# Token lists of the expert slots: scatter and gather through a DRAM table, against indicator matrices summed on TensorE

## The chip, the cores and the metric

The kernel is one program on one core of a Trainium2 chip. The metric is the device time of one execution in microseconds (us). Three executions of the kernel before took 1595.52, 1600.85 and 1601.16 us; their median, 1600.85 us, is the time before.

## The reference

Three layers run one after the other on 8 x 576 = 4608 tokens. Only the third, a routed mixture of eight experts, bears on the change.

```python
def _moe2_ref(x, w_gate, w1, w2):            # x: 4608 x 512, 8 experts, F = 1024
    logits = x @ w_gate
    expert_idx = np.argmax(logits, axis=1)
    ...
    gate_w = probs[np.arange(N), expert_idx]
    for e in range(E):
        mask = expert_idx == e
        xe = x[mask]
        h = np.maximum(xe @ w1[e], 0.0)
        out[mask] = gate_w[mask, None] * (h @ w2[e])
...
x = _attn_ref(q, k, v)                       # block-causal attention, 8 heads
x = _moe_ref(x, w1, w2, w3, w_out)           # ((x @ w1) * (x @ w2)) @ w3 @ w_out
return _moe2_ref(x, moe2_w_gate, moe2_w1, moe2_w2)
```

## The kernel before

The program has three stages: attention with the first half of the dense layer; the rest of the dense layer with the routing (from about 884 to 1090 us of the trace); and the experts (to the end). The order of the instructions is the order in which the Python code issues them; each engine runs its own list in that order and waits on semaphores. DMAs are issued by SP (SyncE, `nc.sync`) and by POOL (GpSimd, `indirect_dma_start`), each a list in program order too.

**Routing stage.** The tokens are taken in nine groups of four tiles of 128. `x2_bank` computes half a tile of the layer's output (24 float32 matmuls into one PSUM bank); ACT copies it to `row`, and `store_x2` writes finished rows to `x2d` in DRAM. `route` finds each token's expert (`oh`, a one-hot), its rank within the expert (two bf16 matmuls with `tri`, into `r`), and from both a position, expert times region plus rank (`posi`). Then it scatters the token numbers `tid` to these positions in four DRAM tables `tab`, one POOL DMA per tile, 36 in all, 4 bytes per token. The tables have been zeroed at the start of the program (`tab<-ti`).

**The held banks.** Eight banks of the last two groups (the `held` list) are kept back, so that TensorE has work while VectorE (DVE) does the last routing. They are called bank 0 to bank 7 here; each is followed by a 256 KB store to `x2d`. `slot_table` runs between them. It counts the tokens of each expert (`cnt`, one matmul), lays the experts out over 25 slots (18 of them pairs, with 256 tokens; 43 units of 128 in all), and makes `widx`, the index for the weights of each slot, and `ui`, the index of each unit's row in the tables. Then it gathers those rows back (`idr<-tab`, four POOL DMAs), transposes and sums them on TensorE (`p`), and writes the token numbers to `ids`.

**Experts.** For each slot, `wload` fetches 2 MB of weights by an indirect DMA with `widx` (`wr`), twice: number 2s for the first layer of slot s, 2s+1 for the second. `rload` gathers the slot's tokens from `x2d` by `ids` (tile `x`). `wsplit` splits the weights into a high part on ACT (`wh`) and a low part on DVE or POOL (`wl`). `xprep` transposes the tokens on TensorE (`t`) and splits them on ACT and DVE (`xhl`). Then TensorE multiplies (`hps`, `yps`), and the result is scattered to the output. The first slot is started in `run`, ahead of the loop.

Of the kernel before, what the change touches and what calls it, by code (L numbers as in the profile page):

```python
# [8 lines left out]
F32 = mybir.dt.float32  # L9
F32R = mybir.dt.float32r  # L10
BF16 = mybir.dt.bfloat16
# [35 lines left out]
def tile_moe_stack(ctx: ExitStack, tc: tile.TileContext, qd, kd, vd, w1, w2, w3t, wo, wg,  # L47
                   e1, e2, c_id, c_msk, c_tri, c_tid, c_row, c_cst, out):
# [11 lines left out]
    NUE = -(-NT // 256) * 2  # L60
    REG = NUE * 128
# [4 lines left out]
    tab = [dram.tile([9 * REG, 1], F32, name=f"tab{j}") for j in range(4)]  # L66
# [5 lines left out]
    one = const.tile([128, 128], F32, name="one")  # L72
    cst = const.tile([128, 16], F32, name="cst")
    crow = const.tile([128, c_row.shape[1]], F32, name="crow")
    tid = const.tile([128, NTILE], F32, name="tid")
# [78 lines left out]
    def attention(sa):  # L154
# [235 lines left out]
        for dst_, src in ((t2, c_tri), (tid, c_tid), (crow, c_row), (cst, c_cst)):  # L390
            nc.sync.dma_start(out=dst_, in_=src)
        NZ = 9 * REG // 128
        ti = ld.tile([128, max(NZ, RW)], F32, name="ti")
# [171 lines left out]
    def route(g, row, lg):  # L565
# [14 lines left out]
        oh = ws.tile([128, 4, 8], BF16, tag="oh", name="oh")[:, :nt]  # L580
# [3 lines left out]
        for j in range(nt):  # L584
# [14 lines left out]
        nc.vector.tensor_tensor(out=rk, in0=ps[:, :8 * nt].rearrange("p (a b) -> p a b", b=8),  # L599
                                in1=cst[:, 8:16].unsqueeze(1).to_broadcast([128, nt, 8]), op=ALU.add)  # L600
        nc.vector.tensor_tensor(out=rk, in0=rk, in1=oh, op=ALU.mult)
# [3 lines left out]
        nc.vector.tensor_copy(out=posi[:, :nt], in_=pos)  # L605
# [12 lines left out]
    def slot_table():  # L618
# [4 lines left out]
        t = ws.tile([U, 8 * NUE], F32, tag="t8", name="t8", bufs=1)  # L623
        v = ws.tile([U, 96], F32, tag="tv", name="tv", bufs=1)
        c8, u8, p8 = v[:, 0:8], v[:, 8:16], v[:, 16:24]
        nc.vector.tensor_copy(out=c8, in_=cnt[0:U, :8])
        t3 = t.rearrange("p (e s) -> p e s", s=NUE)
        nc.vector.tensor_tensor(out=t3, in0=c8.unsqueeze(2).to_broadcast([U, 8, NUE]),
                                in1=crow[0:U, 0:NUE].unsqueeze(1).to_broadcast([U, 8, NUE]), op=ALU.is_gt)
        nc.vector.tensor_reduce(out=u8, in_=t3, axis=AX.X, op=ALU.add)  # L630
        h = NUE // 2
        t4 = t[:, 0:8 * h].rearrange("p (e s) -> p e s", s=h)
        nc.vector.tensor_tensor(out=t4, in0=u8.unsqueeze(2).to_broadcast([U, 8, h]),
                                in1=crow[0:U, NUE:NUE + h].unsqueeze(1).to_broadcast([U, 8, h]), op=ALU.is_ge)
        nc.vector.tensor_reduce(out=p8, in_=t4, axis=AX.X, op=ALU.add)
        sc = ws.tile([U, 2, 24], F32, tag="sc", name="sc", bufs=1)
        nc.vector.memset(sc, 0.0)
        A = sc[:, :, 8:24]
        nc.vector.tensor_scalar(out=A[:, 0, 0:8], in0=p8, scalar1=2.0, scalar2=None, op0=ALU.mult)
        nc.vector.tensor_tensor(out=A[:, 0, 8:16], in0=u8, in1=A[:, 0, 0:8], op=ALU.subtract)  # L640
# [3 lines left out]
        ends = sc[:, 0, 8:24]  # L644
        starts = sc[:, 0, 7:23]
        bs = v[:, 24:40]
        co = crow[0:U, NUE + h:]
        nc.vector.tensor_copy(out=bs[:, 0:8], in_=co[:, 8:16])
        nc.vector.scalar_tensor_tensor(out=bs[:, 8:16], in0=p8, scalar=2.0, in1=co[:, 8:16], op0=ALU.mult, op1=ALU.add)
        nc.vector.tensor_tensor(out=bs, in0=bs, in1=starts, op=ALU.subtract)  # L650
        P2 = sc[:, 0, 15:16]
        tt = v[:, 40:48]
        nc.vector.scalar_tensor_tensor(out=tt[:, 0:1], in0=P2, scalar=0.5, in1=co[:, 17:18], op0=ALU.mult, op1=ALU.min)
        nc.vector.scalar_tensor_tensor(out=tt[:, 1:2], in0=P2, scalar=0.5, in1=co[:, 18:19], op0=ALU.mult,
                                       op1=ALU.is_le)
        nc.vector.tensor_tensor(out=tt[:, 0:1], in0=tt[:, 0:1], in1=co[:, 16:17], op=ALU.add)
        nc.vector.scalar_tensor_tensor(out=tt[:, 0:1], in0=tt[:, 1:2], scalar=1000.0, in1=tt[:, 0:1],
                                       op0=ALU.mult, op1=ALU.add)
        g0, g1 = v[:, 48:64], v[:, 64:80]
        tb = tt[:, 0:1].to_broadcast([U, 16])  # L660
        nc.vector.tensor_tensor(out=g0, in0=starts, in1=tb, op=ALU.is_le)
        nc.vector.tensor_tensor(out=g1, in0=ends, in1=tb, op=ALU.is_le)
        nc.vector.tensor_tensor(out=g0, in0=g0, in1=g1, op=ALU.subtract)
        nc.vector.tensor_tensor(out=bs, in0=bs, in1=tb, op=ALU.add)
        nc.vector.tensor_tensor(out=bs, in0=bs, in1=g0, op=ALU.mult)
        nc.vector.tensor_reduce(out=tt[:, 2:3], in_=bs, axis=AX.X, op=ALU.add)
        nc.vector.scalar_tensor_tensor(out=tt[:, 2:3], in0=g1[:, 15:16], scalar=float(8 * REG // 128),
                                       in1=tt[:, 2:3], op0=ALU.mult, op1=ALU.add)
        ui = ws.tile([U, 1], I32, tag="ui", name="ui", bufs=1)
        nc.vector.tensor_copy(out=ui, in_=tt[:, 2:3])  # L670
        g8 = v[:, 80:96]
        nc.vector.tensor_tensor(out=g8, in0=g0, in1=co[:, 19:35], op=ALU.mult)
        nc.vector.tensor_reduce(out=tt[:, 3:4], in_=g8, axis=AX.X, op=ALU.add)
        nc.vector.scalar_tensor_tensor(out=tt[:, 3:4], in0=g1[:, 15:16], scalar=7.0, in1=tt[:, 3:4],
                                       op0=ALU.mult, op1=ALU.add)
        dg = ws.tile([U, U], F32, tag="dg", name="dg", bufs=1)
        nc.vector.tensor_scalar(out=dg, in0=ident[0:U, 0:U], scalar1=tt[:, 3:4], scalar2=None, op0=ALU.mult)
        used = tt[:, 4:5]
        nc.vector.tensor_scalar(out=used, in0=P2, scalar1=0.5, scalar2=float(NPR), op0=ALU.mult, op1=ALU.min)
        nc.vector.tensor_tensor(out=used, in0=ends[:, 15:16], in1=used, op=ALU.subtract)  # L680
        nc.vector.tensor_copy(out=nuse, in_=used[0:1])
        ir = ws.tile([U, 4, 128], F32, tag="idr", name="idr", bufs=1)
        for j in range(4):
# [200 lines left out]
    with tc.manual_schedule():  # L884
# [140 lines left out]
        for i, h_ in enumerate(held):  # L1025
            x2_bank(*h_)
            store_x2(h_[0], h_[4], h_[1])
            if i == 0:
# [3 lines left out]
                for _ in rt:  # L1032
                    pass
# [85 lines left out]
```

## Time and profile before

| | us |
|---|---|
| median of three executions | 1600.85 |
| the profiled execution | 1599.49 |
| its span, from the first to the last instruction | 1597.7 |
| around the span | 1.8 |
| busy time of PE (TensorE) in the span | 1522.2 |
| busy time of DVE (VectorE) | 972.6 |
| busy time of ACT (ScalarE) | 885.2 |
| busy time of POOL (GpSimd) | 784.8 |

The busy times are sums over stages with different limits. Which engine sets the time of a stage is read from that stage: from its stretch of the windows and from the timelines of the engines there. The granted clock of TensorE has two levels, 2.4 GHz (1.00 in the profile) and 1.2 GHz (0.50).

### The profile page before, as it was taken

Reading aid. Unit: us, or ns where it says so; the run is one execution under the profiler, and the core shown is the slowest. Engines: PE = TensorE matmul, PEld = TensorE weight load, DVE = VectorE, ACT = ScalarE, POOL = GpSimd, SP = SyncE. Lnnn points to the kernel's source line nnn. Section 1 sums busy time; section 2 is a strip of 40 time slices with the busy share of each in tenths; the row PEclk is TensorE's granted clock in tenths of the full one; section 3 lists DMA queues with packets and bytes.
Section 4 is the critical chain, followed back from the end, with each engine's and each line's share of the span. In section 5 each row is a group of like instructions: output and inputs, shape, how many; then the busy total and the mean of one; then the engine's idle time right before and its main releaser. Section 6 shows DMA issues by size and latency. Waiting matters only on the chain. (4 is left out here: it accounts for less than half of the span.)

```text
span 1597.7 us, 28972 instructions
## 1 busy us (share of the span) xinstructions
PE 1522.2 (95%) x10689; PEld 1425.6 (89%) x10689; DVE 972.6 (61%) x2508; ACT 885.2 (55%) x1961; POOL 784.8 (49%) x768
## 2 busy tenths in 40 slices
PE   6888999999999999999999999994999999999996
PEld 3568999999999999999999999994998898898896
DVE  7777666666666666666569243351755766565761
ACT  5586766766676667666435233321644555555551
POOL 4577566566656565564224033233436454645441
PEclk9589999999999999999999999997999999999999
DMA  6523332333232323230464467739166425465240
GB/s 197 145 80 105 86 103 90 98 97 100 86 102 87 103 92 103 88 93 24 154 182 162 85 140 139 146 64 172 48 230 232 175 71 220 162 226 209 105 146 21
DMA packets 59059, 198.31 MB, mean 124 GB/s; under 512 B 10568, under 2 KB 11340, under 8 KB 55330
## 3 DMA queue, kind: packets, MB, share of 16 engines
q1 hardware_dynamic: 45026, 117.87, 27.7%
q0 software_dynamic: 13888, 78.54, 13.8%
q8 instruction: 87, 1.43, 0.4%
q14 instruction: 58, 0.48, 0.1%
HBM read 187.27 MB, written 39.24 MB: 142 GB/s over the span
## 5 line engine op out<-in xcount | busy, mean ns | idle before, releaser
L309 POOL TENSOR_SCALAR P<-P,m 128x512 f32<-128x512 f32 (+4 forms) x288 | 161.9, 563 | 223.0 <-DVE m L308 159.8
L79 DVE TENSOR_TENSOR wl<-wr,wh 128x1024 fp32r<-128x1024 f32 x128 | 219.5, 1741 | 63.3 <-ACT wh L78 44.3
L775 PE MATMUL hps<-xhl,wh 128*128 128x256 f32 x1152 | 207.9, 282 | 3.5 <-ACT xhl L756 2.1
L818 PE MATMUL yps<-wh,hhw 128*128 128x512 f32 x624 | 201.4, 398 | 3.4 <-DVE hhw L780 2.7
L294 DVE CUSTOM_DVE_ANT_0 P<-s,msk 128x512 f32<-128x512 f32 (+2 forms) x320 | 152.0, 482 | 86.4 <-PE t L326 52.6
L78 ACT ACTIVATE wh<-wr 128x1024 fp32r<-128x1024 f32 x168 | 169.8, 1061 | 50.9 <-DMA wr<-e,widx 50.9
L775 PEld LDWEIGHTS hps<-xhl,wh 128*128 128x128 f32 x1152 | 179.8, 190 | 5.7 <-ACT xhl L756 2.5
L302 ACT ACTIVATE P<-P,m 128x512 f32<-128x512 f32 (+4 forms) x288 | 166.8, 579 | 10.2 <-DVE m L294 8.2
L313 DVE TENSOR_TENSOR ptl<-t,pth 128x512 fp32r<-128x512 f32 (+3 forms) x288 | 146.2, 508 | 38.5 <-ACT pth L312 33.2
L775 PE MATMUL hps<-xhl,wl 128*128 128x256 f32 x576 | 163.2, 283 | 2.4 <-POOL wl L79 2.4
L556 PE MATMUL x<-wfh,abh 128*128 128x264 f32 (+1 forms) x576 | 163.4, 284 | 0.0
L556 PE MATMUL x<-wfl,abh 128*128 128x264 f32 (+1 forms) x576 | 162.8, 283 | 0.0
L556 PE MATMUL x<-wfh,abl 128*128 128x264 f32 (+1 forms) x576 | 162.3, 282 | 0.0
L464 ACT ACTIVATE ab<-mm 128x288 f32<-128x288 f32 x128 | 52.7, 411 | 184.9 <-PE mm L458 183.7
L326 PE MATMUL t<-ident,P 128*128 128x128 f32 x768 | 137.6, 283 | 12.9 <-DVE m L307 12.9
L818 PEld LDWEIGHTS yps<-wh,hhw 128*128 128x128 f32 x624 | 116.6, 188 | 32.5 <-DVE hhw L780 5.4
L356 PE MATMUL av<-ptl,VV 128*128 128x256 f32 (+1 forms) x448 | 127.6, 307 | 5.8 <-DVE m L307 5.0
L312 ACT ACTIVATE pth<-t 128x512 fp32r<-128x512 f32 (+3 forms) x288 | 129.4, 449 | 5.0 <-PE t L326 1.8
L356 PE MATMUL av<-pth,VV 128*128 128x256 f32 (+1 forms) x448 | 128.7, 305 | 0.7 <-ACT pth L312 0.7
L326 PEld LDWEIGHTS t<-ident,P 128*128 128x128 f32 x768 | 97.5, 145 | 28.3 <-issue 17.2
L818 PE MATMUL yps<-wl,hhw 128*128 128x512 f32 x312 | 122.7, 393 | 0.0
L780 DVE SCALAR_TENSOR_TENSOR hhw<-hps,hhw 128x512 fp32r<-128x512 f32 x72 | 49.6, 690 | 112.4 <-ACT hhw L779 107.7
(224 smaller groups left out, 4478.0 us busy)
## 6 DMA issues: line engine op xcount, KB each, us to landing
qr<-qd SPq DMA_DIRECT2D x29, 640.0 KB
abT<-ab SPq DMA_DIRECT2D x64, 288.0 KB
abr<-abT SPq DMA_DIRECT2D x36, 512.0 KB
kr<-kd SPq DMA_DIRECT2D x29, 576.0 KB
vr<-vd SPq DMA_DIRECT2D x32, 320.0 KB
str<-w SPq DMA_DIRECT2D x16, 512.0 KB
str<-w3t SPq DMA_DIRECT2D x16, 512.0 KB
x2d<-row SPq DMA_DIRECT2D x7, 1026.0 KB
```

What stands on the lines that cost most here:

```text
L78: nc.scalar.activation(out=hi, in_=src, func=AF.Copy)
L79: (eng or nc.vector).tensor_tensor(out=lo, in0=src, in1=hi.bitcast(F32), op=ALU.subtract)
L294: nc.vector.tensor_tensor_reduce(out=pr[:, o_:o_ + w_], in0=s_, in1=msk[:, c_:c_ + w_], scale=-0.125, scalar=BIG, op0=ALU.add, op1=ALU.min ...
L302: nc.scalar.activation(out=pr, in_=pr, func=AF.Exp, bias=m[:, 0:1], scale=-1.0, accum_out=m[:, 3:4])
L309: nc.gpsimd.tensor_scalar(out=pr, in0=pr, scalar1=m[:, 6:7], scalar2=1.0, op0=ALU.mult, op1=ALU.mult)
L312: nc.scalar.activation(out=dst_h, in_=src, func=AF.Copy)
L313: nc.vector.tensor_tensor(out=dst_l, in0=src, in1=dst_h.bitcast(F32), op=ALU.subtract)
L326: nc.tensor.transpose(t_[:, 128 * c:128 * c + 128], pr[:, 128 * c:128 * c + 128], ident)
L356: nc.tensor.matmul(t_[:, x0:n], lhsT=vv[:, k_, hd, :], rhs=pt[:, hd, o_ + x0:o_ + n], start=(c == 0), stop=(c == 2 * kcs - 1))
L556: nc.tensor.matmul(ps[:, :c1 - c0], lhsT=u[:, k_, j * 128:j * 128 + 128], rhs=w_[:, k_, c0:c1], start=(c == 0), stop=(c == 23))
L775: nc.tensor.matmul(ps[:, d], lhsT=u[:, f2, k_, 128 * d:128 * d + 128], rhs=x[:, k_], start=(c == 0), stop=(c == 11))
L818: nc.tensor.matmul(ps, lhsT=u[:, g, o_], rhs=w_[:, g * 512:g * 512 + 512], start=(c == 0), stop=(c == 23))
```

## The change

The tables in DRAM are gone, with their zeroing, the 36 scatters and the four gathers. `route` now keeps, in SBUF, each token's one-hot (`ohs`), its rank divided by 128 and the remainder (`ubr`), and a 128 x 128 indicator of the remainder per tile (`brow`, bf16). `slot_table` runs on all 128 partitions: it computes `widx` without the matmul `dgs`, then issues the first weight load, and then computes for each token the unit in which it stands (`vk`). In four steps of nine tiles it makes an indicator of token against unit, multiplied by the token's two coordinates (`eq`, two buffers), and TensorE sums these over the tokens with `brow` as weights: 36 bf16 matmuls of 86 columns into one bank, `ids`. Two DVE instructions make `ids` of it. In `run`, the second weight load is issued ahead of the token gathers.

```diff
@@ route
-        posi = ws.tile([128, 4], I32, tag="posi", name="posi")
...
-        for j in range(nt):
-            nc.gpsimd.indirect_dma_start(
-                out=tab[j][:], out_offset=bass.IndirectOffsetOnAxis(ap=posi[:, j:j + 1], axis=0),
-                in_=tid[:, t0 + j:t0 + j + 1], in_offset=None)
+        nc.vector.tensor_copy(out=ubr[:, :, t0:t0 + nt], in_=posi[:, 0:2, :nt])
+        yield
+        nc.vector.tensor_tensor(out=brow[:, t0:t0 + nt], in0=ubr[:, 1, t0:t0 + nt].unsqueeze(2).to_broadcast([128, nt, 128]),
+                                in1=crow[:, 0:128].unsqueeze(1).to_broadcast([128, nt, 128]), op=ALU.is_equal)
@@ slot_table
-        for j in range(4):
-            nc.gpsimd.indirect_dma_start(out=ir[:, j], out_offset=None,
-                                         in_=tab[j][:].rearrange("(r c) o -> r (c o)", c=128),
-                                         in_offset=bass.IndirectOffsetOnAxis(ap=ui[:, 0:1], axis=0))
-        yield
-        ps = ps_m.tile([128, 512], F32, tag="mm", name="dgs")
-        nc.tensor.matmul(ps[:, :NSL], lhsT=one[0:U, :], rhs=dg[:, :NSL], start=True, stop=True)
...
         wload(0)
...
+        nc.vector.tensor_tensor(out=vt, in0=vt, in1=ohs[:, :NTILE], op=ALU.mult)
+        nc.vector.tensor_reduce(out=vk, in_=vt, axis=AX.X, op=ALU.add)
+        nc.vector.tensor_tensor(out=vk, in0=vk, in1=ub, op=ALU.add)
...
         yield
-        p2 = ps_m.tile([128, 512], F32, tag="mm", name="p2")
-        for j in range(4):
-            nc.tensor.matmul(p2[:, :U], lhsT=ir[:, j], rhs=ident[0:U, 0:U], start=(j == 0), stop=(j == 3))
-        nc.vector.tensor_scalar(out=ids, in0=p2[:, :U], scalar1=float(NT), scalar2=None, op0=ALU.add)
+
+        ps = ps_m.tile([128, 512], F32, tag="mm", name="ids")
+        step = -(-NTILE // 4)
+        for a in range(0, NTILE, step):
+            b = min(NTILE, a + step)
+            w_ = b - a
+            eq = ws.tile([128, 2, step, U], BF16, tag="eq3", name="eq3")
+            nc.vector.tensor_tensor(out=eq[:, 1, :w_], in0=vk[:, a:b].unsqueeze(2).to_broadcast([128, w_, U]),
+                                    in1=tt.unsqueeze(1).to_broadcast([128, w_, U]), op=ALU.is_equal)
...
+            for t in range(a, b):
+                nc.tensor.matmul(ps[:, :2 * U].rearrange("p (a u) -> p a u", a=2), lhsT=brow[:, t],
+                                 rhs=eq[:, :, t - a], start=(t == 0), stop=(t == NTILE - 1))
@@ run
+            wload(2 * s0 + 1)
             rload(s0)
-            wload(2 * s0 + 1)
@@ the held banks
-            if i == min(3, len(held) - 1):
-                next(tb)
-            if i == min(7, len(held) - 1):
-                next(tb, None)
-        next(tb, None)
+            if i == min(4, len(held) - 1):
+                next(tb)
+                for _ in tb:
+                    pass
```

POOL's list between the last routing and the first slot, before. `wr` is a weight load, `x` a gather of tokens; the square brackets name the engines and DMA queues whose semaphores the instruction waits for (DMASW: POOL's DMAs, DMAHW: SP's).

```order
L607 DMA tab_62<-tid,posi 41472x1 [waits DMASW7_49]
L684 DMA idr<-tab_59,ui 43x128 [waits DMASW0_49,DVE_49]
L684 DMA idr<-tab_60,ui 43x128 [waits DMASW1_49]
L684 DMA idr<-tab_61,ui 43x128 [waits DMASW2_49]
L684 DMA idr<-tab_62,ui 43x128 [waits DMASW3_49]
L711 DMA wr_11860<-e,widx 128x4096 [waits DVE_49]
L745 DMA x_14415<-x2d,ids 128x513 [waits DMAHW3_49,DMAHW4_49,DMAHW2_49,DMAHW5_49,DMAHW1_49,DMAHW6_49,DMAHW0_49,DMAHW7_49,DVE_49,Pool_49]
L745 DMA x_14417<-x2d,ids 128x513 [waits Activation_49]
L711 DMA wr_14412<-e,widx 128x4096
```

The same stretch of POOL's list in the change.

```order
L73 TENSOR_TENSOR abl<-abr,abh 128x512 [waits DMAHW2_49,Activation_49]
L706 DMA wr_11846<-e,widx 128x4096 [waits DVE_49]
L706 DMA wr_14431<-e,widx 128x4096 [waits PE_49,Activation_49,Pool_49]
L740 DMA x_14437<-x2d,ids 128x513 [waits DMAHW4_49,DMAHW3_49,DMAHW5_49,DMAHW2_49,DMAHW6_49,DMAHW1_49,DMAHW7_49,DMAHW0_49,DVE_49]
L740 DMA x_14439<-x2d,ids 128x513 [waits Activation_49]
L740 DMA x_14441<-x2d,ids 128x513
```

The first weight load has no gather ahead of it any more and waits for DVE alone; the second weight load stands ahead of the token gathers, and waits for TensorE, since its buffer takes the place of a tile that the last held banks read. The first token gather still waits for all stores of `x2d`.

TensorE's list from bank 4 to the first slot in the change; nine pairs of a weight load and a matmul follow each first use of an `eq`.

```order
L694 LDWEIGHTS brow
L694 MATMUL ids<-eq_14261,brow 128x86 [waits DVE_49]
...
L694 MATMUL ids<-eq_14274,brow 128x86 [waits DVE_49]
...
L694 MATMUL ids<-eq_14287,brow 128x86 [waits DVE_49]
...
L694 MATMUL ids<-eq_14300,brow 128x86 [waits DVE_49]
...
L547 MATMUL x<-wfh,abh 128x256 [waits Activation_49]
...
L749 MATMUL t<-ident,x_14437 128x128 [waits DMASW2_49]
```

Before, this stretch of TensorE's list held `dgs` ahead of bank 4, no other instruction between the banks, and after bank 7 the four matmuls `p<-ident,idr` ahead of the first `t`. Now the 36 matmuls stand between bank 4 and bank 5, with four waits for DVE, and nothing stands between bank 7 and `t`.

## Rows read from the trace of the kernel before

**Rows 1.** The page: span, and busy time of TensorE with its share and instructions.
```profile
span 1597.7 us, 28972 instructions
...
PE 1522.2 (95%) x10689; PEld 1425.6 (89%) x10689; DVE 972.6 (61%) x2508; ACT 885.2 (55%) x1961; POOL 784.8 (49%) x768
```

**Rows 2.** Windows of stretches: length, busy us (instructions), granted clock, DMA share, GB/s.
```profile
884.00:1060.00 176.00, 176.00 (x1477) 175.61 (x1476) 65.69 (x223) 57.66 (x133) 48.98 (x42) 1.00 0.60 124
...
1090.00:1100.00 10.00, 0.00 (x0) 0.00 (x0) 0.00 (x0) 0.12 (x1) 5.30 (x4) 0.74 0.83 66
1100.00:1110.00 10.00, 3.54 (x12) 2.71 (x12) 0.80 (x2) 1.69 (x2) 3.88 (x4) 0.50 0.89 284
1110.00:1120.00 10.00, 6.45 (x32) 5.72 (x32) 7.20 (x8) 6.25 (x9) 2.24 (x2) 0.56 0.64 248
1120.00:1130.00 10.00, 10.00 (x84) 9.82 (x83) 8.57 (x9) 6.99 (x10) 5.37 (x4) 1.00 0.21 54
```

**Rows 3.** Timeline of TensorE: start us, us, instruction, count [idle before, releaser].
```profile
1068.92 0.19 PE L593 MATMUL r<-oh,tri 128*128 128x32 bf16 x1
...
1078.06 0.38 PE L556 MATMUL x<-wfh,abh 128*128 128x256 f32 x1
...
1089.42 0.28 PE L556 MATMUL x<-wfh,abl 128*128 128x256 f32 x1
1100.94 0.65 PE L703 MATMUL p<-ident,idr 43*128 43x43 f32 x2 [11.24 <-DMA idr<-tab,ui]
...
1109.07 2.08 PE L754 MATMUL t<-ident,x 128*128 128x128 f32 x8 [4.98 <-DMA x<-x2d,ids]
...
1115.28 0.58 PE L775 MATMUL hps<-xhl,wh 128*128 128x256 f32 x1 [1.47 <-DVE xhl L757]
```

**Rows 4.** Timeline of POOL, the DMAs that it issues.
```profile
1078.72 0.96 POOL L607 DMA_INDIRECT tab<-tid,posi  x1 [0.30 <-issue]
1088.50 1.45 POOL L684 DMA_INDIRECT idr<-tab,ui  x1 [8.82 <-DMA tab<-tid,posi]
...
1097.02 1.42 POOL L684 DMA_INDIRECT idr<-tab,ui  x1 [3.60 <-DMA tab<-tid,posi]
1098.74 1.03 POOL L711 DMA_INDIRECT wr<-e,widx  x1 [0.30 <-DMA x2d<-row]
1105.11 0.99 POOL L745 DMA_INDIRECT x<-x2d,ids  x1 [5.34 <-DVE ids L704]
```

**Rows 5.** Timeline of DVE from the last routing to the first slot.
```profile
1070.60 0.19 DVE L599 TENSOR_TENSOR rk<-r,cst 128x32 f32<-128x32 f32 x1 [1.10 <-PE cnt L621]
...
1071.53 0.45 DVE L628 TENSOR_TENSOR t<-tv,crow 43x288 f32<-43x288 f32 x1
...
1078.82 0.19 DVE L696 SCALAR_TENSOR_TENSOR widx<-dup,crow 128x25 int32<-128x25 f32 x1
1104.13 0.20 DVE L704 TENSOR_SCALAR ids<-p 128x43 int32<-128x43 f32 x1 [25.12 <-PE p L703]
1109.40 4.63 DVE L79 TENSOR_TENSOR wl<-wr,wh 128x1024 fp32r<-128x1024 f32 x4 [5.07 <-ACT wh L78]
1113.95 1.28 DVE L757 TENSOR_TENSOR xhl<-t,xhl 128x512 fp32r<-128x512 f32 x2
```

**Rows 6.** Timeline of ACT at the first slot.
```profile
1108.31 3.90 ACT L78 ACTIVATE wh<-wr 128x1024 fp32r<-128x1024 f32 x4 [18.19 <-DMA wr<-e,widx]
```

**Rows 7.** SP's queue (stores to `x2d`): packets, MB, share, in 1071:1090 and 1099:1101.
```profile
q1 hardware_dynamic: 799, 1.48, 108.2%
...
q1 hardware_dynamic: 50, 0.08, 19.8%
```

**Rows 8.** A short pause of TensorE early on: its timeline, and the window around it.
```profile
141.45 0.41 PE L356 MATMUL av<-ptl,VV 128*128 128x320 f32 x1 [2.18 <-DVE m L307]
...
140.00:150.00 10.00, 8.55 (x53) 8.34 (x54) 6.47 (x24) 6.46 (x19) 6.77 (x8) 0.83 0.27 88
```

**Rows 9.** Timeline of SP's DMA issues at the start of the program.
```profile
8.19 3.12 SPq L404 DMA_DIRECT2D tab<-ti  x4
```

More of the change, by code (lines that the diff above doesn't have):

```diff
@@ L47, in tile_moe_stack @@
 def tile_moe_stack(ctx: ExitStack, tc: tile.TileContext, qd, kd, vd, w1, w2, w3t, wo, wg,
-                   e1, e2, c_id, c_msk, c_tri, c_tid, c_row, c_cst, out):
+                   e1, e2, c_id, c_msk, c_tri, c_row, c_cst, out):
     nc = tc.nc
@@ L71, in tile_moe_stack @@
     tri = const.tile([128, 256], BF16, name="tri")
[L72 to L75, printed above, removed]
+    cst = const.tile([128, 8], F32, name="cst")
     def split(hi, lo, src, eng=None, scale=None):
@@ L401, in attention @@
                 f(0)
-        nc.sync.dma_start(out=x2d[NT:NT + 1, :], in_=ti[0:1, :RW])
-        for t_ in tab:
-            nc.sync.dma_start(out=t_[:].rearrange("(p c) o -> p (c o)", p=128), in_=ti[:, :NZ])
+        nc.sync.dma_start(out=x2d[NT:NT + 1, :], in_=ti)
         nc.scalar.activation(out=tri, in_=t2, func=AF.Copy)
@@ L659, in slot_table @@
[L659 to L666, printed above, removed]
@@ L676, in slot_table @@
[L676 to L682, printed above, removed]
@@ L691, in slot_table @@
+        tt = tt[:, 0]
+        g1 = ws.tile([128, NSL, 16], F32, tag="t8", name="t8", bufs=1)
+        nc.vector.tensor_tensor(out=g1, in0=ends.unsqueeze(1).to_broadcast([128, NSL, 16]),
+                                in1=tt[:, :NSL].unsqueeze(2).to_broadcast([128, NSL, 16]), op=ALU.is_le)
+        es = ws.tile([128, 2, NSL + 1], F32, tag="es", name="es", bufs=1)
+        e_, dup = es[:, 0], es[:, 1, 0:NSL]
         nc.vector.memset(e_[:, 0:1], -1.0)
-        nc.vector.tensor_copy(out=e_[:, 1:NSL + 1], in_=ps[:, :NSL])
@@ L704, in slot_table, with by_expert @@
-        nc.vector.tensor_scalar(out=ids, in0=p2[:, :U], scalar1=float(NT), scalar2=None, op0=ALU.add)
+        df = v[:, 32:40]
+        nc.vector.tensor_tensor(out=df, in0=starts[:, 8:16], in1=starts[:, 0:8], op=ALU.subtract)
+        nc.vector.tensor_tensor(out=df, in0=df, in1=p2, op=ALU.subtract)
+        vt = ws.tile([128, NTILE, 8], F32, tag="t8", name="vt", bufs=1)
+        vk = ws.tile([128, NTILE], F32, tag="vk", name="vk", bufs=1)
+        ub = ubr[:, 0, :NTILE]
+        def by_expert(a):
+            return a.unsqueeze(1).to_broadcast([128, NTILE, 8])
@@ L707, in tile_moe_stack @@
+        yield
+        idf = ws.tile([128, 2, U], F32, tag="idf", name="idf", bufs=1)
+        nc.vector.tensor_scalar(out=idf[:, 0], in0=ps[:, U:2 * U], scalar1=128.0, scalar2=float(NT), op0=ALU.mult, op1=ALU.add)
+        nc.vector.tensor_tensor(out=ids, in0=ps[:, 0:U], in1=idf[:, 0], op=ALU.add)
     rawt, wset = [], []
@@ L885, in tile_moe_stack @@
         ps_m = pool(sm_, "ps_m", 3, space=PSUM)
-        nc.gpsimd.memset(one, 1.0)
         nc.gpsimd.memset(base[:, 0], 0.0)
@@ L993, in tile_moe_stack @@
         ws = pool(sx, "ws", 2)
+        br = pool(sx, "br", 1)
+        ohs = br.tile([128, NG * 4, 8], BF16, name="ohs")
+        ubr = br.tile([128, 2, NG * 4], F32, name="ubr")
+        brow = br.tile([128, NTILE, 128], BF16, name="brow")
+        crow = br.tile([128, c_row.shape[1]], F32, name="crow")
+        nc.sync.dma_start(out=crow, in_=c_row)
         ng = len(groups)
```

130 lines of the change are left out of this document (57 added, 73 removed).

## The prediction

> **What bounds the kernel now.** I read the page first. TensorE is busy 95% of the span [rows 1], so time is to be won only where it stands still or runs at half rate. The windows show where that is near the change: in 884 to 1060 us TensorE is busy in every microsecond, with DVE at 65.7 and POOL at 49.0 of 176; in 1090 to 1120 it works 10 of 30 us, and the granted clock falls to 0.50, that is 1.2 GHz, and is back at 1.00 only in the window that begins at 1120 [rows 2]. So the routing stage is bound by TensorE, and the passage from the last held bank to the first slot is a hole.
>
> The timelines show what the hole is made of. TensorE ends bank 7 at 1089.70 (1089.42 and 0.28), waits 11.24 us for the gathered table rows, transposes them, waits 4.98 us for the tokens, and gets steady work from 1115.28, after one more wait, for the low part of the tokens on DVE [rows 3]. That is 25.6 us from end to steady start. On POOL the last scatter is issued at 1078.72, the first gather of a table row waits 8.82 us for an earlier scatter to land and goes at 1088.50, the last one waits until 1097.02; behind them in POOL's list stand the first weight load (1098.74) and, after `ids` (1104.13 on DVE, rows 5), the token gather at 1105.11 [rows 4]. `widx`, all that the weight load needs, was ready at 1079.01 [rows 5]; the load stood 19.7 us in a queue. The weights reach ACT at 1108.31 [rows 6], 9.6 us after their issue, and DVE's four `wl` (4.63 us from 1109.40) push its two `xhl` to 1113.95 [rows 5]. Removing the scatters and gathers thus removes two links of the chain; the question is which link is late next.
>
> **Part by part.** I write E for the end of bank 7 on TensorE, 1089.70 now.
>
> *Routing, nine groups.* POOL loses 36 scatters, DVE gains per group one `brow` (128x512; `xhl` of that shape takes 0.64 us, rows 5) and two more small instructions, together some 9 us over the stage. TensorE covers both: it is busy all the time there while DVE has 110 us free [rows 2]. Worth 0. Without that cover the price would be those 9 us.
>
> *DVE from the last routing to `ids`.* Before, 43 instructions run from 1070.60 to 1079.01 [rows 5], 8.4 us, four of them wide (128x288-like rows take 0.45 us); without the wide ones' extra of 0.8 and a short wait of 0.3 that is 0.17 us each. Now 32 instructions lead to `widx`, two of them of 400 elements (some 0.55 us): 30 x 0.17 + 2 x 0.55 = 6.2, so `widx` at 1076.8. The first weight load goes then, 22 us earlier than now. Next come 11 instructions for `vk` and the count of slots, five of them of 288 elements: 6 x 0.17 + 5 x 0.45 = 3.3, to 1080.1; `brow` of the last group, 0.64, to 1080.7; and four steps of three instructions of 387 elements, by their size 0.53 each and so 1.5 a step: `eq` is ready at 1082.2, 1083.7, 1085.2 and 1086.7.
>
> *TensorE among the held banks.* The 36 matmuls stand behind bank 4, which ends at 1080.7 (start at 1078.06, 2.9 us a bank, less 0.3 since `dgs` is gone) [rows 3]. So it waits for each `eq`, the last at 1086.7, and adds nine matmuls. No row has such a matmul of 86 columns; the nearest, bf16 with 32 columns, takes 0.19 [rows 3]; unpipelined, nine take 1.7 us, fully overlapped almost nothing; I take 0.9. Bank 5 starts at 1087.6 instead of 1081.0: 6.6 us later. What waits behind is banks 5 to 7 and their stores. The pause is also a threat to the clock: the nearest case is the wait of 2.18 us at 139 to 141, after which the window has a clock of 0.83, a third of 10 us at half rate, or 1.7 us lost [rows 8]. Bounds 0 and 3.4 (twice that); I take 1.7. So E = 1089.7 + 6.6 + 1.7 = 1098.0.
>
> *After E.* Gone are `p` and its wait. The weights of the first slot have had 20 us to land, twice their 9.6 now, so ACT can split them right after its copy of bank 7, and DVE follows: 1.1 + 4.63 us after that, done by E + 6.5. The token gather needs `ids` (early) and all stores of `x2d`. Now the last store cannot go before bank 7's end at 1089.70; its queue still moves packets in 1099 to 1101, after 799 packets held it at 108% of the 16 engines in 1071 to 1090 [rows 7]: the stores lag, and the last lands some 10 us after E. In the change, TensorE's pause gives the queue 6.6 us to catch up, and the scatters are gone, but the weight loads share the engines. Bounds: 3 us after E (no lag) and 10 (as now); I take 6.5. The gather then goes at E + 6.7 and TensorE starts `t` 3.96 us later, as now (1105.11 to 1109.07), at E + 10.7. The second weight load, now ahead of the gather in the queue and free to go at E, gives the same by its own route: 9.6 us to land and about 1 for the gather behind it. From `t` to steady `hps`: the eight transposes take 2.08 us [rows 3], then half of an ACT `xhl` pair and a DVE half of 0.64; 3.3 in all, where now it is 6.2, because `wl` is out of the way. Steady start at E + 14.0 = 1112.0, against 1115.28: **3.3 us won**. The half clock at its start stays as it is, since the hole remains. The next thing in line, the second weights, comes earlier than now and so holds nothing up.
>
> *Start of the program.* Four table writes took 3.12 us of SP's list at 8.19 [rows 9], with weight and value loads behind them; two constant loads go too. DVE is then the busy engine, so most of this is hidden: bounds 0 and 3, I take 1.
>
> Sum: 3.3 + 1 = 4.3 us. The profiled execution took 1599.5, so 1595.2; the median lies 1.4 higher, in a spread of 5.6 over three runs, and I say **1595.5**. Half a per cent, 8 us, is about what a measurement of this kernel can tell from no change.
>
> **A rule against it.** A scatter that POOL had issued long before 1088.50 still held up the gather until then, while the stores crept [rows 4, 7]. The Trainium skill, "DMA: Bandwidth & Descriptors", section "Queues, rings and completion order", says that a DMA's semaphore increment lands only after every earlier write of that engine, across its queues; the same page, "Issuing engines are not separate DMA queues", that all issuing engines share 16 DMA engines and interleave. By that rule the waits of these rows have the stores as their cause, and they go with the stores, not with the tables: the second weights and the tokens would be as late after E as the stores make them. That is the second rival.
>
> **The rivals.**
> 1. *The pause is cheap and the stores land at once.* The clock holds (E = 1096.3), the store lands 3 us after E, and `t` is bound by the second weights and starts at E + 9.5; steady start at E + 12.8 = 1109.1, 6.2 won, and up to 3 at the start: 1590. For it: the pause lets the queue drain. Against: the clock of rows 8.
> 2. *The stores take over the wait.* The last store lands 10 us after E as now; gather at E + 10.2, `t` at E + 14.2, steady at E + 17.5 = 1115.5: nothing won, 1599. For it: rows 7, and the weight loads that now run beside the stores. Against: the pause.
> 3. *Slower: the clock falls in the pause and stays at half through banks 5 to 7.* Those take 2.9 us each at full rate, so 8.7 more: E = 1105.0, steady start 1119.0, 3.7 lost and nothing won at the start, 1603; with the slow landing of rival 2, 1607. It decides from the point where the pause, its clock and a landing later than 6.5 us cost over 11.6 us together (25.6 us of hole now, less the 14.0 after E). For it: half clock from a wait of 2.18 us in rows 8, here there are four waits. Against: each wait after the first is some 1.5 us with work between. The skill's "TensorE: Matmul & The Clock Gate", section "HAM oscillation — how this bites in real kernels", describes such waits between short bursts of matmuls as the pattern that puts the clock back to half again and again; the price above is from the rows.
> 4. *Nothing to be seen:* gains at the start lost to a different clock there. It is contained in the spread of the others.
>
> **How the numbers follow.** Forecast (1592 to 1598) 0.50; rival 1 (1587 to 1592) 0.22; rival 2 (1598 to 1601) 0.18; rival 3 (1601 to 1610) 0.10. The range leaves out the better fifth of rival 1 and most of rival 3: 1588 to 1602. Faster by over 0.5% means under 1592.8: all of rival 1 and little of the forecast, 0.26; slower by over 0.5% means over 1608.9, the end of rival 3, 0.05; 0.69 between.
>
> **What would show it.** On POOL the first `wr` at about 1077 instead of 1098.7 (relative to the routing's end), no `tab` and `idr`. On DVE `widx` 6 to 7 us after the last `rk`, and 1.5 us a step for `eq`. On TensorE a broken stretch of 6 to 7 us between bank 4 and bank 5, and a window there with a clock below 1; then a hole of about 14 us instead of 25.6, ended by `x`, and no `wl` between `t` and `hps`. I am wrong on the step if the hole is under 11 us (rival 1) or over 17 (rival 2), and on the pause if bank 5 starts less than 4 or more than 10 us after bank 4. The whole prediction is wrong if the time comes from elsewhere: from the start, or from slots beyond the first.

## The result, and the profile after

The change takes 1583.24 us (median of four executions, 1582.51 to 1589.28), the kernel before, run beside it, 1601.01 (four, 1595.52 to 1605.88). The ratio is 0.9898, with a 95% interval of 0.9858 to 0.9939. The forecast was 1595.5, with a range of 1588 to 1602: the time is 12 us under the forecast and outside the range.

The profiled execution took 1582.65 us, with a span of 1580.9. I cut both spans at three instructions: the last routing's `r` on TensorE, the end of the first slot's second `xhl` on DVE (steady start), and the last DMA that POOL issues. The second stretch, from `r` to steady start, is called the passage from here on.

| stretch | before | after | won |
|---|---|---|---|
| start to `r` | 1068.9 | 1059.8 | 9.2 |
| `r` to steady start | 46.3 | 42.3 | 4.0 |
| steady start to POOL's last issue | 471.4 | 473.5 | -2.0 |
| POOL's last issue to the end | 11.0 | 5.4 | 5.7 |

The prediction priced the first stretch at 1 us and the second at 3.3. It put the slots at nothing, with the second weights as the reason, and did not mention the end. The page and the windows after (columns as in [rows 1, 2]):

```profile
span 1580.9 us, 28995 instructions
...
PE 1516.8 (96%) x10715; PEld 1422.6 (90%) x10715; DVE 976.9 (62%) x2546; ACT 883.8 (56%) x1961; POOL 744.0 (47%) x727
```

```profile
884.00:1060.00 176.00, 175.99 (x1474) 175.46 (x1473) 68.72 (x262) 55.40 (x130) 16.74 (x13) 1.00 0.50 118
...
1060.00:1070.00 10.00, 9.99 (x85) 9.99 (x85) 8.87 (x45) 1.49 (x4) 1.46 (x1) 1.00 0.33 103
1070.00:1080.00 10.00, 6.86 (x64) 6.41 (x63) 6.67 (x17) 0.38 (x1) 0.00 (x0) 0.76 0.65 241
1080.00:1090.00 10.00, 8.15 (x61) 7.94 (x60) 0.46 (x1) 2.58 (x5) 1.00 (x1) 0.90 0.19 74
1090.00:1100.00 10.00, 1.25 (x6) 1.25 (x7) 4.18 (x4) 2.44 (x4) 5.17 (x5) 0.61 0.93 314
1100.00:1110.00 10.00, 9.17 (x57) 8.48 (x56) 7.93 (x8) 6.72 (x9) 2.46 (x2) 0.70 0.03 7
```

In the routing stage TensorE is as busy as before, with DVE 3 us busier (9 predicted) and POOL 32 us less. The pause shows in 1070 to 1080, with a clock of 0.76, and 1110 is already past the hole. The timeline of TensorE:

```profile
1059.76 0.19 PE L584 MATMUL r<-ohs,tri 128*128 128x32 bf16 x1
...
1072.35 0.52 PE L694 MATMUL ids<-eq,brow 128*128 128x86 bf16 x9 [0.69 <-DVE eq L691]
1073.78 0.52 PE L694 MATMUL ids<-eq,brow 128*128 128x86 bf16 x9 [0.91 <-DVE eq L691]
1075.21 0.80 PE L694 MATMUL ids<-eq,brow 128*128 128x86 bf16 x9 [0.91 <-DVE eq L691]
1076.64 0.81 PE L694 MATMUL ids<-eq,brow 128*128 128x86 bf16 x9 [0.63 <-DVE eq L691]
1077.23 0.56 PE L547 MATMUL x<-wfh,abh 128*128 128x256 f32 x1
...
1082.31 0.28 PE L547 MATMUL x<-wfh,abh 128*128 128x256 f32 x1
...
1087.87 0.28 PE L547 MATMUL x<-wfh,abl 128*128 128x256 f32 x1
1098.75 1.97 PE L749 MATMUL t<-ident,x 128*128 128x128 f32 x8 [10.60 <-DMA x<-x2d,ids]
```

Each group of nine matmuls waits for its `eq`; bank 7 ends at 1088.15 (that is E), and the hole, from E to steady start, has one wait, 10.60 us for the tokens, where there were two of 11.24 and 4.98 [rows 3]. POOL, DVE and ACT in the same stretch:

```profile
1067.28 1.46 POOL L706 DMA_INDIRECT wr<-e,widx  x1 [37.21 <-DVE tv L661]
1088.98 1.00 POOL L706 DMA_INDIRECT wr<-e,widx  x1 [20.25 <-ACT row L551]
1092.57 1.31 POOL L740 DMA_INDIRECT x<-x2d,ids  x1 [2.59 <-DVE wl L73]
```

```profile
1060.39 0.16 DVE L590 TENSOR_TENSOR rk<-r,ohs 128x32 f32<-128x32 f32 x1
...
1066.80 0.19 DVE L656 SCALAR_TENSOR_TENSOR widx<-es,crow 128x25 int32<-128x25 f32 x1
...
1070.80 0.54 DVE L687 TENSOR_TENSOR eq<-vk,tt 128x387 bf16<-128x387 f32 x1
...
1076.02 0.56 DVE L691 TENSOR_TENSOR eq<-eq,crow 128x387 bf16<-128x387 bf16 x1
...
1089.55 4.63 DVE L73 TENSOR_TENSOR wl<-wr,wh 128x1024 fp32r<-128x1024 f32 x4 [11.63 <-ACT wh L72]
...
1101.39 0.69 DVE L752 TENSOR_TENSOR xhl<-t,xhl 128x512 fp32r<-128x512 f32 x1 [0.16 <-ACT xhl L751]
```

```profile
1071.70 0.38 ACT L551 ACTIVATE row<-x 128x256 f32<-128x256 f32 x1 [2.46 <-PE x L547]
1082.51 0.39 ACT L551 ACTIVATE row<-x 128x256 f32<-128x256 f32 x1 [10.42 <-PE x L547]
1085.35 0.38 ACT L551 ACTIVATE row<-x 128x256 f32<-128x256 f32 x1 [2.46 <-PE x L547]
1088.19 0.38 ACT L551 ACTIVATE row<-x 128x256 f32<-128x256 f32 x1 [2.46 <-PE x L547]
1088.47 3.88 ACT L72 ACTIVATE wh<-wr 128x1024 fp32r<-128x1024 f32 x4
```

The first weight load goes at 1067.28, as soon as `widx` is there; ACT splits the weights right behind the copy of bank 7. The copies of bank 4 and bank 5 are 10.81 us apart, where neighbours are 2.84 apart: the pause and its clock cost 8.0 us. Bank 5 starts at 1077.23 and bank 6 at 1082.31; these 5.08 us instead of 2.84 make 2.2 of the 8.0 the clock, and the pause itself 5.7. Next, SP's queue of stores in 1062:1081 and at its end in 1090:1092, and all that moves in 1092:1099:

```profile
q1 hardware_dynamic: 578, 1.05, 14.4%
```

```profile
q1 hardware_dynamic: 38, 0.05, 6.1%
```

```profile
q0 software_dynamic: 352, 2.60, 90.7%
```

Before, 799 packets of stores took 108.2% of the 16 engines over 19 us [rows 7], about 0.41 us each (1.082 x 16 x 19 / 799); now 578 take 14.4%, 0.076 us each. POOL's own packets beside the stores, four scatters and the first gather of table rows, took next to nothing in that stretch of the kernel before (1071:1090):

```profile
q0 software_dynamic: 132, 0.00, 0.5%
```

The last store's packets are gone by E + 2.1, where before they still moved 10 us after E. From then on only POOL's queue moves: tokens and second weights.

Last, what no step of the prediction covered: the end of the program, POOL's last row before and after.

```profile
1586.66 0.98 POOL L825 DMA_INDIRECT out_dram<-y,ids  x1 [4.63 <-ACTq L872]
```

```profile
1575.55 0.98 POOL L820 DMA_INDIRECT out_dram<-y,ids  x1 [4.62 <-ACTq L867]
```

From these to the ends of the spans it is 11.0 us before and 5.4 after. The traces also hold what POOL runs there, which the timelines leave out: behind its last waits an instruction named DRAIN, of 5.71 us before and 1.22 after, and just ahead of it one named INC_SWDGE_SEM, of 1.57 and 0.47 us. These two make 5.6 of the 5.7 us.

### The profile page after: what moved, and what is told of

Its sections match the earlier page's. It is cut to its first block, busy times and chain, and to the rows that moved or that the text cites. A ratio compares the mean times of both kernels' runs of the same rounds, so it can differ in the third digit from the quotient of the medians.

```text
span 1580.9 us, 28995 instructions
## 1 busy us (share of the span) xinstructions
PE 1516.8 (96%) x10715; PEld 1422.6 (90%) x10715; DVE 976.9 (62%) x2546; ACT 883.8 (56%) x1961; POOL 744.0 (47%) x727
## 3 DMA queue, kind: packets, MB, share of 16 engines
q0 software_dynamic: 12288, 78.42, 13.9%
q8 instruction: 87, 1.43, 0.4%
## 5 line engine op out<-in xcount | busy, mean ns | idle before, releaser
L73 DVE TENSOR_TENSOR wl<-wr,wh 128x1024 fp32r<-128x1024 f32 x128 | 214.4, 1700 | 71.0 <-ACT wh L72 70.9
L296 ACT ACTIVATE P<-P,m 128x512 f32<-128x512 f32 (+4 forms) x288 | 166.7, 579 | 11.1 <-DVE m L288 9.4
## 6 DMA issues: line engine op xcount, KB each, us to landing
x2d<-row SPq DMA_DIRECT2D x7, 1026.0 KB, 10.5
```

What stands on the lines that cost most here:

```text
L73: (eng or nc.vector).tensor_tensor(out=lo, in0=src, in1=hi.bitcast(F32), op=ALU.subtract)
L296: nc.scalar.activation(out=pr, in_=pr, func=AF.Exp, bias=m[:, 0:1], scale=-1.0, accum_out=m[:, 3:4])
```

## The experiments

Each run is given by its median, the ratio to the kernel before run beside it, and its stretches.

**Both kernels again**, unchanged.

> The kernel before, unchanged, profiled and timed again. The change gained 16.8 us of span, which by the two traces splits into 9.2 up to the last routing, 3.8 in the hole before the first slot, minus 1.9 in the later slots and 5.7 after the last multiplication. Theory A (chance of the execution): the 9.2 are half-clock stretches in the first 150 us and the 5.7 a drain of POOL that varies from one execution to the next; then this run shows other half-clock stretches or a drain near 1.2 us, and its runs spread over 1590 to 1606 us. Theory B (the change's own): the zeroing of the tables and the 40 DMAs of POOL cause both; then this run shows half clock from about 44 to 85 us and a drain near 5.7 us again, and its times stay near 1601.

> The changed kernel, unchanged, as the base for what follows. Theory A: its start and its end vary too, times from 1580 to 1592, a drain of 1.2 or of 5.7 us. Theory B: 1583 in every run, start and drain as in its first profile.

Before: 1599.56 us, ratio 0.9989 [0.9967, 1.0012]; change: 1586.29, 0.9907 [0.9881, 0.9933]. The change's stretches repeat (`r` at 1059.7, 42.1 us to steady start, 5.5 at the end). Those of before don't all: `r` at 1065.0, and 49.5 us to steady start instead of 46.3, since the tokens came 6.5 us after their gather instead of 4.0; 11.1 at the end. So the profile that I predicted from had a short passage.

**The zeroing back in the change**: the tables are zeroed and `tid` is loaded as before; nothing reads them.

```diff
+        for t_ in tab:
+            nc.sync.dma_start(out=t_[:].rearrange("(p c) o -> p (c o)", p=128), in_=ti[:, :NZ])
```

> The change, with the start as before: the tables in DRAM are zeroed and the token numbers loaded, and nothing uses them. Theory A: as the change, 1583 within 2 us. Theory B for the start: 9 us slower, 1592, with half clock in the first 100 us of the trace. My forecast's term for the start was 1 us: 1584.

1588.37 us, 0.9911 [0.9885, 0.9938]; full clock from 71.4 us on, passage 41.7, end 5.1. The profile is that of the change and the ratio is its repeat's, so no cost of the zeroing is seen; a cost of 1 or 2 us would not be seen either (the executions of this run average 1587.1, the ten of the change and its repeat 1585.7).

**The scatters back too**: 36 scatters to the same positions as before, with four small DVE instructions a group for them; nothing reads the tables.

```diff
+        for j in range(nt):
+            nc.gpsimd.indirect_dma_start(
+                out=tab[j][:], out_offset=bass.IndirectOffsetOnAxis(ap=po2[:, j:j + 1], axis=0),
+                in_=tid[:, t0 + j:t0 + j + 1], in_offset=None)
```

> As e3, and also the 36 scatters of POOL into the tables, which nothing reads (with four more small DVE instructions a group). Theory A for the end: drain as in e2, and 1 to 2 us more in the hole. Theory B for the end: a drain near 5.7 us, 4.5 us slower than e3. If the scatters' small writes are what slows the stores of x2d, the token gather goes later than in e3 by up to 6 us.

1602.32 us, 1.0003 [0.9983, 1.0023]: with scatters that nobody waits for the time is that of the kernel before again. POOL's timeline and the stores' queue over the 19 us that answer to those above (1066:1085):

```profile
1081.30 0.95 POOL L617 DMA_INDIRECT tab<-tid,po  x1 [0.30 <-issue]
1095.62 1.04 POOL L723 DMA_INDIRECT wr<-e,widx  x1 [13.37 <-ACT row L558]
1104.45 0.98 POOL L757 DMA_INDIRECT x<-x2d,ids  x1 [7.79 <-issue]
...
1585.90 0.98 POOL L837 DMA_INDIRECT out_dram<-y,ids  x1 [4.62 <-ACTq L884]
```

```profile
q1 hardware_dynamic: 538, 0.99, 36.6%
```

A store packet takes 0.21 us instead of 0.076. The last store lands at E + 7.2 instead of E + 2.1, and the gather behind the stores goes at E + 9.7 instead of E + 4.3 to 4.9 (E is 1094.8 here). Against the run with the zeroing alone, `r` comes 3.2 us later (TensorE is busy 8.00 of 10 us in 1060 to 1070, where the change has 9.99), the passage takes 6.0 more (47.8), and the end 4.1 more (9.2): together with 0.7 in the slots the 14 us between the two.

The total is that of the kernel before, but its parts are not. Before, TensorE had no idle time in 884 to 1060 [rows 2]; the 3.2 us at `r`, where TensorE now waits 1.45 us for `ohs` on DVE, come only with scatters and the new work of DVE together. Of the 6.0 us in the passage 3.0 lie ahead of E and 3.0 behind it (steady start at E + 17.2 instead of E + 14.2), and only those behind E stand where the stores and the token gather do. So this run shows that the scatters slow the stores and lengthen the end; it does not price what the change won.

**The scatters at another place**: the zeroing and 36 scatters to fixed positions, nine in each of the first four groups, so that none stands beside the last stores.

```diff
+        if g < 4:
+            for j in range(9):
+                c_ = 9 * g + j
+                nc.gpsimd.indirect_dma_start(
+                    out=tab[c_ % 4][:], out_offset=bass.IndirectOffsetOnAxis(ap=tii[:, c_:c_ + 1], axis=0),
```

> The change, with the zeroing, and with 36 scatters of POOL into the unused tables, but nine in each of the first four routing groups, at fixed places, long before the held banks. If the cost at the end (POOL's drain, 1.22 us with 120 indirect DMAs, 4.16 with 156 and 5.71 with 160) goes with the number of POOL's DMAs, the drain is 4 us again and the time 4 to 5 us above the change. If it goes with when they run, it is 1.2. If the scatters slow the stores of x2d only where both run at once, the last store lands 2 us after bank 7 as in the change and not 7 as in e4, and the passage to the first slot is that of the change: 1591 in all. A third theory, that scatters anywhere cost what e4 shows: 1601.

1641.42 us, 1.0228 [1.0200, 1.0256]. The total tells nothing, because of a side effect that I had not foreseen: POOL also makes some of the splits `abl` that TensorE reads, nine scatters in a row hold those up, and `r` comes 49 us late. TensorE waits 37.4 of these 49 us directly for POOL, and its clock is at 0.80 to 0.90 in 915 to 1060. Its matmuls on `abl` (matmuls, busy us, mean ns, idle before and releaser):

```profile
L555 PE MATMUL x<-wfh,abl 128*128 128x264 f32 (+1 forms) x576 | 169.1, 294 | 37.4 <-POOL abl L78 37.4
```

Its other stretches do tell. The last store lands at E + 2.1 and the passage takes 42.3 us, as in the change: scatters slow the stores only while they run beside them. The end takes 9.2 us (span 1640.9), as with the 36 late scatters: that part goes with their number, wherever they stand.

```profile
1631.68 0.98 POOL L836 DMA_INDIRECT out_dram<-y,ids  x1 [4.63 <-ACTq L883]
```

**18 scatters**, three in each of the second to the seventh group, otherwise as the last one.

```diff
-        if g < 4:
-            for j in range(9):
-                c_ = 9 * g + j
+        if 1 <= g < 7:
+            for j in range(3):
+                c_ = 3 * g + j
```

> The kernel with the zeroing back, with 18 scatters of 4 bytes per token that nothing reads, three in each of the second to the seventh group, so that none stands beside the last stores: 138 DMAs on POOL. Theory A (the end of the program grows with the number of POOL's DMAs): from TensorE's last matmul to the end 7.5 to 9 us, between the change's 6.5 and the 10.2 of 156 DMAs; all other stretches as in the change (r to the first slot 42 us, last store 2 us after bank 7), time 1585 to 1589. Rival B (the end is long only from some number on, or only when the last scatters are late): 6.5 us as in the change, or over 10.

1589.69 us, 0.9933 [0.9912, 0.9953]; passage 41.3. Its last row, with a span of 1584.7:

```profile
1577.30 0.98 POOL L836 DMA_INDIRECT out_dram<-y,ids  x1 [4.63 <-ACTq L883]
```

The end takes 7.4 us, between 5.1 with none and 9.2 with 36: 2.3 us for 18 scatters, 4.1 for 36. POOL's DRAIN is 1.22 us with none, 2.69 with 18 and 4.16 with 36, early or late: 1.47 us more for each 18. The medians can't show this: another variant with the zeroing and no scatter, run beside this one, took 1589.57 (the rows' constants, below).

**The tokens ahead of the second weights in the change.**

```diff
-            wload(2 * s0 + 1)
             rload(s0)
+            wload(2 * s0 + 1)
```

> The change, with the second weight load behind the token gathers again, as before. In the change the gather goes 4.4 us after bank 7 and TensorE has the tokens 6.2 us later, against 4.0 before the change. If the weights ahead in the queue cost these 2 us: tokens at +8.5 instead of +10.6, the first slot 2 us earlier, 1 to 2 us in the time unless the second weights are then late for the second layer. If they cost nothing: the same time within 1 us.

1583.62 us, 0.9888 [0.9856, 0.9920]. The gather goes when it went (E + 4.2), but `t` starts 4.0 us later instead of 6.2:

```profile
1095.67 1.57 POOL L740 DMA_INDIRECT x<-x2d,ids  x1 [23.68 <-DVE wl L73]
...
1098.80 1.00 POOL L706 DMA_INDIRECT wr<-e,widx  x1 [0.30 <-issue]
```

```profile
1099.69 1.11 PE L749 MATMUL t<-ident,x 128*128 128x128 f32 x4 [8.19 <-DMA x<-x2d,ids]
1101.27 1.12 PE L749 MATMUL t<-ident,x 128*128 128x128 f32 x4 [0.47 <-DMA x<-x2d,ids]
```

The passage is 40.7 us. That is 1.4 to 1.6 us less than in the change's two profiles; the time cannot tell it from the change.

**No pause**: the 36 matmuls in two halves, behind bank 5 and bank 6, where their `eq` are there already. In `slot_table` the four steps become two pairs, with a `yield` ahead of each pair's matmuls; the calls in the held banks follow:

```diff
-            if i == min(4, len(held) - 1):
-                next(tb)
-                for _ in tb:
-                    pass
+            if i in (4, 5):
+                next(tb)
+            if i == 6:
+                for _ in tb:
+                    pass
```

> The change, with the 36 matmuls in two halves, behind bank 5 and behind bank 6, so that each finds its indicators ready. My forecast put the pause behind bank 4 at 6.6 us, and the trace of the change at 7.6. If the held banks set when the last store and the second weights go, bank 7 ends 5 to 6 us earlier and so does the first slot: 1580. If the stores of x2d set it, they lag again without the pause, the last lands 5 us or more after bank 7, and half of this or more is lost.

1579.99 us, 0.9871 [0.9846, 0.9896]. The matmuls have no wait ahead of them, and the copies of the banks stand 3.64 us apart:

```profile
1074.20 0.89 PE L699 MATMUL ids<-eq,brow 128*128 128x86 bf16 x18
1077.84 0.89 PE L699 MATMUL ids<-eq,brow 128*128 128x86 bf16 x18
```

```profile
1070.00:1080.00 10.00, 10.00 (x109) 9.91 (x109) 6.68 (x16) 1.15 (x3) 0.00 (x0) 1.00 0.81 292
1080.00:1090.00 10.00, 1.64 (x14) 1.43 (x13) 4.63 (x4) 4.16 (x5) 3.89 (x4) 0.75 0.68 232
```

The clock stays at 1.00 to the end of bank 7, which comes 22.0 us after `r` instead of 28.4; the stores still land at E + 2.1, and the passage is 35.7. The pause did not help the stores: without it E comes 6.4 us earlier, and the passage is 6.4 to 6.6 us shorter. Not all of it reaches the end of the program. The slots take 475.9 us instead of 473.1 to 473.5, most of it in the wait for the low weights on POOL (6.2 us of idle time of TensorE instead of 4.2 to 4.3), and the medians are 3.3 and 6.3 us under the change's two, with intervals that overlap.

**No pause and the tokens first**, both edits.

> The change with the 36 matmuls in two halves, behind bank 5 and bank 6, and the second weight load behind the token gathers again. If the gain of each holds beside the other, r to the first slot is 35.7 less 1.5, about 34 us, and the time 1577 to 1580, 3 to 6 us under the change. If the tokens don't come earlier there, since the weights then set the start, 35.7 us and the time 1580 as without the pause alone.

1577.39 us, 0.9855 [0.9834, 0.9877], the lowest median of all; passage 34.1. Its interval overlaps that of the run without the pause alone. Its first window belongs to the question of the start, below.

**The first weights ahead of the table gathers, in the kernel before.**

```diff
         wload(0)
+        for j in range(4):
+            nc.gpsimd.indirect_dma_start(out=ir[:, j], out_offset=None,
```

> The kernel before, with one thing changed: the first weight load stands ahead of the four gathers of table rows in POOL's list. If the weights' late issue alone made the hole, tokens and their split follow in 3.3 us instead of 6.2, and the hole is 3 us shorter: 1598. If the table rows and tokens set it, and the 2 MB now run ahead of them in the same engines, the rows arrive later and the gain is 0 or a loss. The end is as before, drain 5.7 us.

1602.69 us, 1.0000 [0.9980, 1.0020]. The load goes at E - 9.3 instead of E + 9, and nothing is won: the last store lands at E + 18.6 instead of E + 10.9, the tokens start at E + 24.4, and the passage takes 49.9. While the scatters are there, weights that come early don't shorten the passage (49.5 and 49.3 in two of the three profiles without this edit), and the stores land later.

**The rows' constants at either place.** The change also moves the load of `crow` out of the start. In one run it is put back there (with the zeroing), in the other it is moved out of the kernel before.

```diff
-((t2, c_tri), (tid, c_tid), (cst, c_cst))
+((t2, c_tri), (tid, c_tid), (crw, c_row[:, 0:90]), (cst, c_cst))
```

> The kernel with the zeroing back (of the third run), with the load of the constant rows (90 columns on 128 partitions, read by nothing) put back at its old place in the start, between the other constants. Theory A (the old start's loads hold TensorE's first work back): the half clock of the start lasts to about 84 us again instead of 71 to 72, the last routing's r comes about 5 us later (1064 to 1065 instead of 1059.7), and the time is 1591 to 1594. Rival B (the start's clock is not set by what is loaded there): half clock to 71 or 72 us, r at 1059 to 1061, time 1584 to 1588 as the change.

> The kernel before, with the load of the constant rows taken out of the start and put ahead of the routing stage. Theory A (that load is what makes the start's half clock last): half clock to 71 or 72 us instead of 84, r at about 1060, time 5 us under before, 1595 to 1597. Rival B (it is not): half clock to 83 or 84 us, r at 1064 to 1069, time 1599 to 1602 as before.

1589.57 us, 0.9938 [0.9916, 0.9960], and 1600.11, 1.0011 [0.9991, 1.0031]: neither is told apart from its kernel. What they show is the clock of the start. Window 72:84 of the kernel before, of the change, of the kernel before with the load moved out, of the change with all loads of the old start put back, and of the change without pause and with the tokens first, in this order:

```profile
72.00:84.00 12.00, 12.00 (x33) 7.24 (x34) 5.85 (x25) 7.21 (x19) 5.24 (x6) 0.50 0.17 55
```

```profile
72.00:84.00 12.00, 11.49 (x57) 6.93 (x56) 10.46 (x42) 10.89 (x30) 8.71 (x11) 1.00 0.19 59
```

```profile
72.00:84.00 12.00, 11.79 (x56) 6.97 (x56) 10.57 (x41) 10.96 (x30) 8.31 (x11) 1.00 0.18 55
```

```profile
72.00:84.00 12.00, 11.49 (x58) 7.15 (x58) 10.65 (x42) 11.13 (x30) 8.92 (x11) 1.00 0.21 61
```

```profile
72.00:84.00 12.00, 12.00 (x33) 7.11 (x32) 5.67 (x25) 7.04 (x17) 5.24 (x6) 0.50 0.18 55
```

At half clock TensorE is busy throughout and issues 33 matmuls, at full clock 56 to 58. The kernel before, with one load moved, can have the full clock there (then `r` is at 1061.0), the change can have it with all the old loads (`r` at 1060.8), and a version of the change can start as the profile of before did (`r` at 1068.7). So the 9.2 us of the first row of the table are not shown to be work that the change removed: in these rows they go with the clock that the one and the other execution got. How often each kernel gets which is left open below.

## Why the prediction was wrong

**What bounds the kernel, and which link comes next: right.** The hole shrank because the two links were removed, and the tokens were next.

**DVE and the pause: right.** `widx` was ready 6.6 us after the start of the last `rk` (6.2 predicted), an `eq` step 1.43 us (1.5, though three times the 0.53 that I wrote is 1.6), nine matmuls 0.52 to 0.81 (0.9), pause and clock 8.0 us (8.3), steady start E + 13.9 (14.0). Two of these agree by luck: the pause was 5.7 us (6.6) and its clock 2.2 (1.7), and the parts behind E cancel as the next paragraph says. The sum was 3.3 us, the two profiles give 4.0.

**The stores: the size was wrong, and another error hid it.** I took the last store at E + 6.5 from bounds of 3 and 10; it landed at E + 2.1, under the lower one. The bounds came from the stores as they ran beside scatters, and I counted on the pause for the queue's catching up as much as on the scatters' absence. The runs with the scatters back (E + 7.2), with the scatters elsewhere and without the pause (E + 2.1 both) show that the scatters slowed the stores and the pause did nothing for them. The gather then went at E + 4.4 instead of 6.7, but the tokens took 6.2 us instead of 3.96, since 2 MB of second weights were ahead of them, as the run with the tokens first shows. So `t` came at E + 10.6 (10.7 predicted), by the route of rival 1. What I drew from [rows 4, 7] was therefore turned the wrong way: the stores did not creep by themselves, the scatters made them. The Trainium skill, "DMA: Bandwidth & Descriptors", "Issuing engines are not separate DMA queues", has all issuers share the 16 engines; the 0.21 us a packet with the scatters beside the stores, against 0.076 without, agree with it as far as that the one queue slows the other. The size does not follow from it: POOL's packets in that stretch of the kernel before took 0.5% of the 16 engines, and how so few bytes hold up the stores is not shown. Rival 2, which I built on that page, fell with the scatters.

**The price of the old passage came from one short execution.** Before took 46.3 us in the profile that I worked from, 49.5 in its second, and 49.3 with the constants' load moved; the change 42.3 and 42.1, and 41.7 and 41.2 with loads put back. The means differ by 6.5 us, not by 3.3.

**The start: my 1 us is not shown, and the clock there is far larger.** The executions average 1585.7 us in the change and its repeat, 1587.1 with the zeroing back and 1589.1 with all loads back; their spread of some 10 us can't tell these apart, so a cost of 1 to 3 us is neither shown nor excluded. What differed between the two profiles is rival 4's clock, which I took as contained in the spread of the other rivals; it is 9 us.

**The step that failed is the sum itself: it stops at the first slot.** The end of the program gained 5.7 us, more than all terms of the forecast, and it was in no step: I priced POOL's 40 DMAs only in the routing and in the hole, and the runs show a price at the end that goes with their number. The slots, which I put at nothing because the second weights come earlier, lost some 2: TensorE's idle time ahead of the low weights that POOL makes grew by 1.9 (row of before, then of after).

```profile
L775 PE MATMUL hps<-xhl,wl 128*128 128x256 f32 x576 | 163.2, 283 | 2.4 <-POOL wl L79 2.4
```

```profile
L770 PE MATMUL hps<-xhl,wl 128*128 128x256 f32 x576 | 163.7, 284 | 4.3 <-POOL wl L73 4.3
```

The other profiles agree (2.3 and 2.4 with the old passage, 3.9 to 5.6 with the new); why POOL's part is later there is not shown. Of the 12.5 us by which the two spans differ beyond my 4.3, then, 5.7 are the end, 0.7 the passage, -2.0 the slots, and 8.2 the start, where the windows show the clock that the two executions got. With the same clock in both starts the spans would differ by 7.6 us, and the miss would look small although the end was still in no step.

**Rival 3 fell.** After the waits of the pause the clock was at half for one stretch (0.76 in 1070 to 1080, 0.90 in the next), which took in bank 5 (0.41 to 0.42 us a matmul, against 0.28), not banks 6 and 7, whose copies are 2.84 us apart. The pattern that the Trainium skill describes in "TensorE: Matmul & The Clock Gate", "HAM oscillation — how this bites in real kernels", did not come back again and again here. The waits there are for DMAs and several times as long as the four here, which were under 1 us each.

**The sum as it should have been.** Passage 6.5, end 5.8, slots -1.8 (means of three profiles with the old passage and end, and of four with the new): 10.5 us. All executions of these kernels average 1601.0 (85 of before, its repeat and the one with the load moved) and 1587.0 (22 of the change, its repeat and the two with loads put back), 14.0 us apart. Some 3.5 us stay open. `r` came at 1068.9, 1065.0 and 1061.0 in the three profiles of the old kind and at 1059.7 to 1061.0 in the four of the new; whether the change makes the better start likelier, or these executions drew it by chance, no run decides. Executions of the new kind reach 1592 to 1593 us too, at a mean clock of 0.976 to 0.979, and their four profiles are all of executions of 1582.2 to 1583.6 us.

## What to carry to other kernels

Price a removed DMA at three places: where something waits for it, where it runs beside other transfers, and at the end of the program; here the end alone was worth more than the whole forecast. Carry the sum from the first instruction to the last, and take the price of a passage from several profiles, since here one execution was 3 us off in a passage of 48 and 9 us off in its clock at the start. Work of TensorE that DVE prepares goes into the list where its last operand is ready, not where its first one is. And a run that brings the old time back has not shown the old parts: compare stretch by stretch.

## What the runs showed of the hardware

- The time from POOL's last DMA to the end of the program grew with the number of DMAs that POOL had issued: 5.1 to 5.6 us with 120 of them, 7.4 with 138, 9.2 with 156 (twice, early or late ones), 11.0 to 11.1 with 160, four of those being gathers of table rows. Most of the growth is in one DRAIN of POOL, the same to 0.01 us in every profile of a count: 1.22 us with 120, 2.69 with 138, 4.16 with 156, 5.71 with 160, some 0.08 us for each scatter. Whether it goes with the DMAs or with the rows that they move is not shown.
- Scatters of 4 bytes per partition, 36 of them, made the 256 KB stores beside them take 0.21 us a packet instead of 0.076, though they moved hardly any bytes. In the kernel before it is 0.41. Why twice as much is not shown: its first gather of table rows goes only at 1088.50, at the end of the stretch that was read.
- The granted clock in the first 150 us differs from execution to execution of nearly the same instructions: 0.50 or 1.00 in 72 to 84 us, and `r` between 1059.6 and 1068.9 (without the two runs whose 36 scatters held `r` back).
